# An efficient-attention kernel and two MLPs: the first attention units and MLP block 0 written in a list scheduler's order

## The chip, the core and the metric

The kernel runs on one core of one Trainium2 chip, as one program that the host launches once. The time is device microseconds of that core. Before the change it is 1768.31 us, the median of three runs (1767.80 to 1768.87).

## What is computed

Attention over 8 batches, 8 heads, 576 positions and 64 channels gives 4608 tokens of 512 channels; two gated MLPs (512 to 2048 to 512) follow.

```python
def _attn_ref(q, k, v):
    q_s = np.exp(q - np.max(q, axis=-1, keepdims=True))
    q_s = q_s / (np.sum(q_s, axis=-1, keepdims=True) + 1e-09)
    k_s = np.exp(k - np.max(k, axis=2, keepdims=True))
    k_s = k_s / (np.sum(k_s, axis=2, keepdims=True) + 1e-09)
    kv = np.einsum('bhsd,bhse->bhde', k_s, v)
    return np.einsum('bhsd,bhde->bhse', q_s, kv)

def _moe_ref(x, w_in, w_out):      # first MLP
    h = x @ w_in
    return (h * np.clip(h + 3.0, 0.0, 6.0) / 6.0) @ w_out

def _moe2_ref(x, w_in, w_out):     # second MLP
    h = x @ w_in
    return (h * (1.0 / (1.0 + np.exp(-h)))) @ w_out
```

## The kernel before

**Tiling.** The 4608 tokens are nine blocks of 512. Each MLP (a phase, `ph` 0 and 1) goes over the nine blocks `j`, and in each over sixteen slices `f` of 128 of the 2048 hidden channels: 288 steps `n` in all. A step is `mm1` (12 matmuls 128x512 into a PSUM tile `h`), `gate` on ScalarE and VectorE, and `mm2` (12 matmuls into the four accumulators `y0` to `y3`). The loop issues `mm2` one step late, so that PE has `mm1` of step n, then `mm2` of step n-1, while the gate of step n runs.

**Three products for one.** Every matmul operand is split into an upper part in fp32r and the remainder, and three products are summed. So each operand needs a ScalarE copy (upper) and a VectorE subtraction (lower): `gate` does it for g (L414, L415), `x_upper` and `x_lower` for x (L371, L376), and class `Conv` for the weights. A `Conv` of a raw 512 KB weight tile is two ScalarE multiplications (`begin`, L111 and L113, which write `fa` and `fr`), three VectorE operations on the bits (`bits`, L117, L121, L122), the ScalarE copy (`upper`, L136) and the VectorE subtraction (`lower`, L140). Block 0 of the first MLP needs 32 of them, a w_in and a w_out slice for each of its sixteen steps.

**Attention units.** A unit `u` is one block of tokens and one pair of heads; four units make the x of a block. A unit passes seven stages: `q_max` (L298) and `k_max` (L219 to L221), `q_sub` on GpSimd (L306) and `k_turn` on PE (L226), `k_diag`, `k_spread`, `q_exp`, `q_sum` (L321 to L323), `q_norm` on GpSimd (L328), `k_sub` (L247), `k_exp` (L257), `q_turn`, `q_upper` and `q_lower` (L336, L341, L346), `kv_mm`, `kv_sum`, `kv_upper`, `kv_lower` (L267, L275, L284, L290), `x_mm` (L361), `x_upper`, `x_lower`.

**What sets the order.** All is written in a manual schedule: each engine runs its instructions in the order in which the program issues them, and the framework adds only the waits for data and for free buffers. Units 0 to 3 are issued in a first loop (`for t in range(NP + 2)`, L505) that works on three units at a time, each one stage behind the next; the first three `Conv` and the first `mm1` stand at its end. Then the loop over steps (L564) issues, for each step, fixed pieces of the units that are due (`begin`, L549: units 4 to 7 begin at steps 0, 3, 6 and 9), the two `Conv` for step f + 2 while `ph == 0 and j == 0`, `mm1`, `gate`, and `mm2` of the step ahead. Both `Conv` of a step are begun at its start and ended (`upper`, `lower`) behind its gate. Loads go through SP's queue: five pairs of weight tiles at the start, later one pair per step, between the q, k and v of the units.

**Buffers.** `wts` holds sixteen w_in and sixteen w_out tiles. Its buffers first take the raw tiles of slices 0 to 12 and the q, k and v of units 2 and 3 (`early`, L463 to L472); a split tile takes the place of the oldest. Raw tiles 13 to 15 pass through the pool `raw` of two. `t2k` has six buffers of 2 KB for `fa`, `fr`, `r` and others, `g` two, `h` two, `pa` two.

## Time and profile before

| | |
|---|---|
| median of the runs | 1768.31 us |
| the profiled execution | 1766.78 us, its span 1765.1 us, the remaining 1.7 us lie outside the span |
| mean granted clock of TensorE | 0.987 of full speed |
| PE / PEld busy | 96% / 79% of the span |
| DVE / ACT / POOL busy | 45% / 34% / 4% |
| DMA | 125 MB, 71 GB/s over the span |

A row of a group of instructions gives line, engine, operation, the tile written and those read, the shape, and the count; behind the bar the busy time in us and the mean of one in ns; behind the second bar how long the engine stood idle just before them, and what ended it. A row of a timeline begins with the start and the duration in us from the start of the span. DVE is VectorE, ACT is ScalarE, POOL is GpSimd, SP is the engine that issues most DMAs; PEclk is the granted TensorE clock, where 1.00 is 2.4 GHz.

### The profile page before, as it was taken

To read this page: it belongs to the slowest core of one execution; us is meant where nothing else is said; L and a number is where in the kernel's file an instruction comes from. 1 tells how busy PE (TensorE), PEld (TensorE's weight loads), DVE (VectorE), ACT (ScalarE), POOL (GpSimd) and SP (SyncE) were. 2 spreads that over 40 slices of the span, in tenths; PEclk is the share of its full clock that TensorE was granted. 3 is DMA by queue.
4 is the path that set the end of the run, shared out by engine and by line. 5 is a ranking of instruction groups with operands and counts; after the bars stand their busy time and mean duration, and the time that the engine had idled before them with its cause. 6 is when DMAs were issued, how large, how long until landed. Compare 5 with 4: busy or idle time off the path is not lost.

```text
span 1765.1 us, 20277 instructions
## 1 busy us (share of the span) xinstructions
PE 1690.0 (96%) x7984; PEld 1386.6 (79%) x7984; DVE 801.5 (45%) x1450; ACT 600.9 (34%) x1046; POOL 76.8 (4%) x82
## 2 busy tenths in 40 slices
PE   3678899999999999999999999999999999999998
PEld 2456788888888888888888888888888888888887
DVE  6788655556565656555432323232323232332322
ACT  2555444444343434433322322222222222222222
POOL 2000000000000000000000000000000000000000
PEclk9888999999999999999999999999999999999999
DMA  9051522323232323312055201010101010101000
GB/s 282 31 182 32 147 81 81 105 86 105 80 110 81 114 84 104 98 60 78 25 193 201 84 1 48 1 48 1 48 1 48 1 48 1 48 1 48 9 16 24
DMA packets 108319, 125.06 MB, mean 71 GB/s; under 512 B 48320, under 2 KB 82112, under 8 KB 108224
## 3 DMA queue, kind: packets, MB, share of 16 engines
q1 hardware_dynamic: 105824, 123.17, 22.1%
q8 instruction: 63, 1.03, 0.2%
q10 hardware_dynamic: 2400, 0.59, 0.2%
q14 instruction: 32, 0.26, 0.0%
HBM read 88.08 MB, written 35.65 MB: 70 GB/s over the span
## 4 chain that ended last, share of the span: by engine, by line
PE 89%; DVE 6%; ACT 2%; DMA 2%; issue 1%; ACTq 0%; SPq 0%; DVEq 0%
PE h L391 43%; PE y L431 22%; PE y L429 20%; PE pa L361 2%; DVE fa L121 1%; PE pa L267 1%; DVE fa L122 1%; PE pa L336 1%; ACT fa L111 0%; DMA kbuf<-in_k_dram 0%; DVE r L404 0%; DVE fa L117 0%; DVE wo L140 0%; DVE g L415 0%; DMA qraw<-in_q_dram 0%
## 5 line engine op out<-in xcount | busy, mean ns | idle before, releaser
L391 PE MATMUL h<-x,wi 128*128 128x512 f32 x3456 | 847.9, 394 | 0.0
L391 PEld LDWEIGHTS h<-x,wi 128*128 128x128 f32 x3456 | 649.2, 190 | 135.8 <-DVE wi L140 0.4
L429 PE MATMUL y<-g,wo 128*128 128x512 f32 x1728 | 425.6, 396 | 0.1
L431 PE MATMUL y<-wo,g 128*128 128x512 f32 x1728 | 414.9, 389 | 0.0
L431 PEld LDWEIGHTS y<-wo,g 128*128 128x128 f32 x1728 | 324.4, 188 | 67.3
L429 PEld LDWEIGHTS y<-g,wo 128*128 128x128 f32 x1728 | 323.6, 190 | 67.7 <-ACT g L414 0.5
L409 DVE TENSOR_TENSOR r<-r,h 128x512 f32<-128x512 f32 x144 | 99.1, 688 | 455.3 <-ACT r L408 455.3
L415 DVE TENSOR_TENSOR g<-r,g 128x512 fp32r<-128x512 f32 x288 | 199.4, 692 | 146.5 <-ACT g L414 133.9
L414 ACT CAST g<-r 128x512 fp32r<-128x512 f32 x288 | 179.4, 623 | 250.8 <-DVE r L404 142.2
L408 ACT ACTIVATE r<-h 128x512 f32<-128x512 f32 x144 | 86.5, 601 | 468.2 <-PE h L391 468.2
L404 DVE SCALAR_TENSOR_TENSOR r<-r,h 128x512 f32<-128x512 f32 x144 | 98.8, 686 | 263.2 <-ACT r L403 263.2
L403 ACT ACTIVATE r<-h 128x512 f32<-128x512 f32 x144 | 86.3, 600 | 258.8 <-PE h L391 247.8
L361 PE MATMUL pa<-qT,kv 128*128 128x512 f32 (+7 forms) x192 | 40.7, 347 | 24.7 <-DVE kv L290 13.2
L121 DVE CUSTOM_DVE_ANT_0 fa<-fa,fr 128x1024 uint16<-128x1024 uint16 x64 | 53.7, 839 | 9.2 <-ACT r L403 0.5
L361 PEld LDWEIGHTS pa<-qT,kv 128*128 128x128 f32 x192 | 33.0, 207 | 30.3 <-ACT kv L284 12.2
L328 POOL TENSOR_TENSOR qe<-qe,qs 128x512 f32<-128x512 f32 x36 | 37.8, 1050 | 397.8 <-DVE qs L323 386.7
L306 POOL TENSOR_TENSOR qe<-qraw,qm 128x512 f32<-128x512 f32 x34 | 35.7, 1050 | 366.8 <-issue 287.7
L117 DVE TENSOR_SCALAR fa<-fa 128x512 uint32<-128x512 uint32 x64 | 29.4, 459 | 40.0 <-ACT fa L111 40.0
L257 ACT ACTIVATE ke<-ke 128x640 f32<-128x640 f32 x32 | 23.7, 741 | 58.8 <-DVE ke L247 58.8
L371 ACT CAST x<-pa 128x512 fp32r<-128x512 f32 x36 | 21.2, 588 | 38.3 <-PE pa L361 38.2
L284 ACT ACTIVATE kv<-pa,rs 64x64 fp32r<-64x64 f32 x56 | 17.5, 312 | 47.6 <-DVE rs L276 47.3
L267 PEld LDWEIGHTS pa<-vbuf,ke 128*64 128x64 f32 (+1 forms) x560 | 20.8, 136 | 12.2 <-issue 6.7
(80 smaller groups left out, 697.8 us busy)
## 6 DMA issues: line engine op xcount, KB each, us to landing
wd<-sp SPq DMA_DIRECT2D x32, 512.0 KB, 3.0
wi_raw<-in_moe_w_in_dram SPq DMA_DIRECT2D x19, 512.0 KB, 4.7
wo_raw<-in_moe_w_out_dram SPq DMA_DIRECT2D x19, 512.0 KB, 4.2
yd<-o SPq DMA_DIRECT2D x36, 256.0 KB, 2.7
yr<-yd SPq DMA_DIRECT2D x36, 256.0 KB, 3.0
out_dram<-o SPq DMA_DIRECT2D x36, 256.0 KB, 3.3
wi<-wd SPq DMA_DIRECT2D x16, 512.0 KB, 4.2
wo<-wd SPq DMA_DIRECT2D x16, 512.0 KB, 4.2
```

The lines of the kernel that those rows point to most:

```text
L121: nc.vector.tensor_tensor(out=au, in0=au, in1=self.r, op=ALU.add)
L267: nc.tensor.matmul(pk[d, 0 : D + 1], t[0:n, j, d], tv[0:n, j, h, :], start=(j == 0), stop=(j == KCH),)
L361: nc.tensor.matmul(pv[:, :, p0 : p0 + n], w[:, a, :], qT[:, c, :, p0 : p0 + n], start=(n_ == 0), stop=(n_ == 2),)
L391: nc.tensor.matmul(h, w[:, a, c, :], x[:, e, c, :], start=(c == 0 and n == 0), stop=(c == NC - 1 and n == 2),)
L403: nc.scalar.activation(r, h, AF.Relu, bias=3.0)
L404: nc.vector.scalar_tensor_tensor(out=r, in0=r, scalar=6.0, in1=h, op0=ALU.min, op1=ALU.mult)
L408: nc.scalar.activation(r, h, AF.Sigmoid)
L409: nc.vector.tensor_tensor(out=r, in0=r, in1=h, op=ALU.mult)
L414: nc.scalar.copy(g[:, 0], r)
L415: nc.vector.tensor_tensor(out=g[:, 1], in0=r, in1=f32(g[:, 0]), op=ALU.subtract)
L429: nc.tensor.matmul(y[c], w[:, a, cs], g[:, e, :], start=st, stop=sp)
L431: nc.tensor.matmul(y[c], g[:, e, cs], w[:, a, :], start=st, stop=sp)
```

## The change

The part of the program up to the last gate of block 0 is no longer written out as two loops. `first_block` makes a list of jobs (engine, assumed duration, priority, what it must wait for, which buffers it takes and gives back), and `Plan.run` goes through an assumed clock and puts out, at each moment and for each engine, the free job with the lowest key. The kernel's instructions are then issued in that order; no wait is added to hold an engine to the plan. The plan holds a tag `port`, which keeps POOL's tensor operations and certain DVE operations apart in its assumed time. `Conv.bits` and `gate` are cut into single operations so that they can be placed apart, and the loop over steps begins at step 16.

All 32 raw weight tiles now have a place in `wts`, so that each is split into the tile it lies in, and their loads stand in SP's queue without a step's work between them. The q, k and v of units 2 and 3 lie in `ahead`, the second buffer of the x tiles, which is free until x of block 1 is written. The same operations are done on the same data, with the same number of DMAs.

```diff
-        def bits(self):
+        def shift(self):
             au = self.a.bitcast(U32)
             nc.vector.tensor_scalar(
                 out=au, in0=au, scalar1=3, scalar2=None, op0=ALU.logical_shift_left
             )
+        def round(self):
+            au = self.a.bitcast(U32)
             nc.vector.tensor_tensor(out=au, in0=au, in1=self.r, op=ALU.add)
+        def sign(self):
+            au = self.a.bitcast(U32)
             nc.vector.scalar_tensor_tensor(
                 out=au, in0=self.high, scalar=0x80000000, in1=au,
                 op0=ALU.bitwise_and, op1=ALU.bitwise_or,
             )
+        def bits(self):
+            self.shift()
+            self.round()
+            self.sign()
...
+    class Gate:
+        def __init__(self, s):
+            self.s = s
+        def relu(self):
+            self.h = hp.pop(self.s)
+            self.r = tmp.tile([P, BLK], F32, tag="t2k", name="r")
...
-    EARLY = NF - 3
-    for u in range(2, NP):
-        kbuf[u] = wts.tile([P, 2, KCH + 1, D], F32, tag="wi", name="k_early")
-        vbuf[u] = wts.tile([P, KCH + 1, 2, D + 1], F32, tag="wo", name="v_early")
-        early["q", u] = wts.tile(
-            [P, 2, NCH, D], F32, tag="wi" if u % 2 else "wo", name="q_early"
-        )
-    for f in range(EARLY):
+    KB, VB, QB = 2 * (KCH + 1) * D, (KCH + 1) * 2 * (D + 1), 2 * NCH * D
+    ahead = xs.tile([P, 2 * NC * BLK], F32, tag="x", name="ahead")
+    for i, u in enumerate(range(2, NP)):
+        o = i * (KB + VB + QB)
+        kbuf[u] = ahead[:, o : o + KB].rearrange("p (h j d) -> p h j d", h=2, d=D)
+        vbuf[u] = ahead[:, o + KB : o + KB + VB].rearrange("p (j h d) -> p j h d", h=2, d=D + 1)
+        early["q", u] = ahead[:, o + KB + VB : o + KB + VB + QB].rearrange(
+            "p (h i d) -> p h i d", h=2, d=D
+        )
+    for f in range(NF):
...
+    class Plan:
+        PORT = "port"
+        def __init__(self, **tags):
+            self.jobs, self.tags = [], dict(tags, port=1)
+        def add(self, eng, us, key, fn, deps=(), take=(), give=(), port=False):
+            self.jobs.append(
+                (eng, us, key, fn, [d for d in deps if d is not None], list(take), list(give), port)
+            )
+            return len(self.jobs) - 1
...
+                for i in sorted(ready, key=lambda i: jobs[i][2]):
+                    eng, us, key, fn, deps, take, give, port = jobs[i]
+                    if at[i] > now + 1e-9 or busy.get(eng, 0.0) > now + 1e-9:
+                        continue
+                    need = take + ([self.PORT] if port else [])
+                    if any(self.tags[t] < need.count(t) for t in need):
+                        continue
+                    for t in need:
+                        self.tags[t] -= 1
+                    stop = now + us
+                    busy[eng] = stop
+                    if port:
+                        gives.append((stop, [self.PORT]))
+                    if eng in ("SP", "AQ"):
+                        fn, size = fn
+                        dma = max(dma, stop + 1.9) + size / 235e3
+                        stop = dma
+                    if give:
+                        gives.append((stop, give))
+                    end[i] = stop
+                    order.append(fn)
...
+    def first_block():
+        plan = Plan(a=2, h=2, g=2, qe=1, qT=1, ke=1, dg=1, m1=1, t2k=6, q=2, **{f"y{c}": 1 for c in range(NC)})
...
+            qm = add("DVE", 0.7, key(0), lambda: q_max(u), [n_q[u]])
+            km = add("DVE", 1.05, key(0), lambda: k_max(u), [n_k[u]], ["m1", "t2k"], ["t2k"], True)
+            if until <= 1:
+                return
+            kt = add("PE", 0.45, key(1), lambda: k_turn(u, pool), [km], [bank], ["m1"])
+            kd = add("DVE", 0.6, key(1), lambda: k_diag(u), [kt], ["dg"], [bank])
+            qs = add("POOL", 1.05, key(1), lambda: q_sub(u, nc.gpsimd), [qm], [qe], [], True)
...
+            mm = add(
+                "PE", 1.5, key(4), lambda: kv_mm(u, y_psum(u) if small else a_pool),
+                [kx, n_v[u]], [pkb], ["ke"],
+            )
+            kvmm[u] = mm
...
+        plan.tags["ke"] = 2
+        s0 = -30.0
+        load(0, s0, "k")
+        load(0, s0 + 0.1, "q")
+        load(0, s0 + 0.2, "v", "AQ")
+        load(1, s0 + 0.3, "k")
+        load(1, s0 + 0.4, "q")
+        load(1, s0 + 0.5, "v", "AQ")
+        for u in range(2, NP):
+            for i, what in enumerate("kqv"):
+                load(u, s0 + u + 0.1 * i, what)
+        for u in range(NP):
+            unit(u, lambda r, u=u: -20.0 + u - 0.01 * r)
...
+        raws, split = {}, {}
+        for f in range(NF):
+            for o in range(2):
+                raws[o, f] = add(
+                    "SP", 0.55, -10.0 + 0.9 * f + 0.4 * o + (0 if f < 4 else 3.0),
+                    (lambda f=f, o=o: load_w(0, f, o), 524288),
+                )
+        for f in range(NF):
+            for o in range(2):
+                c = Conv(0, f, o)
+                key = f - (1.6 if o else 2.2)
+                c0 = add("ACT", 1.35, key, c.begin, [raws[o, f]], ["t2k", "t2k"])
+                c1 = add("DVE", 0.45, key, c.shift, [c0], port=True)
+                c2 = add("DVE", 0.7, key, c.round, [c1], [], ["t2k"], True)
+                c3 = add("DVE", 0.72, key, c.sign, [c2], port=True)
+                c4 = add("ACT", 0.65, key, c.upper, [c3])
+                split[o, f] = add("DVE", 0.7, key, c.lower, [c4], [], ["t2k"], True)
...
+        for u in (NP, NP + 1):
+            loads(u, -6.5 + (u - NP) * 0.5)
+            unit(u, lambda r, u=u: begin[u] + r + 0.3)
...
+                m = add(
+                    "PE", 0.78, f - 0.5, lambda s=s, c=c: mm1(s, [c]),
+                    [split[0, f], xlow[c], m], ["h"] if c == 0 else [],
+                )
+            g = Gate(s)
+            g0 = add("ACT", 0.62, f - 0.45, g.relu, [m], ["t2k"])
+            g1 = add("DVE", 0.7, f - 0.45, g.times, [g0], [], ["h"])
+            g2 = add("ACT", 0.64, f - 0.45, g.upper, [g1], ["g"])
+            g3 = add("DVE", 0.7, f - 0.45, g.lower, [g2], [], ["t2k"], True)
+            if f < NF - 1:
+                last = add(
+                    "PE", 3.1, f + 0.55, lambda s=s: mm2(s), [g3, split[1, f], last],
+                    [f"y{c}" for c in range(NC)] if f == 0 else [], ["g"],
...
+        for i in range(2):
+            add("SP", 0.55, 14.0 + 0.5 * i, (lambda i=i: load_w(1, 0, i), 524288))
+        for fn in plan.run():
+            fn()
...
-        for u in range(NP):
-            load_q(u)
-            load_k(u)
-            load_v(u, nc.scalar if u < 2 else nc.sync)
...
+        first_block()
...
-        prev = None
-        for n, s in enumerate(steps):
+        prev = steps[NF - 1]
+        for n, s in list(enumerate(steps))[NF:]:
...
-            if ph == 0 and j == 0 and f + 2 < NF:
-                convs = [Conv(0, f + 2, 0), Conv(0, f + 2, 1)]
-            elif ph == 0:
+            if ph == 0:
...
-                if j == 0:
-                    if f + 5 < NF:
-                        load_w(0, f + 5, 0)
-                        load_w(0, f + 5, 1)
-                    if f >= NF - 2:
-                        load_w(1, 0, f - NF + 2)
```

**Places where the order moves.** The first is the start of the program on VectorE: the kernel before, from the first attention operation on (m is `k_max`, mx and dg `k_diag`, qs `q_sum`, ke `k_sub`, rs `kv_sum`; the numbers tell the buffers apart):

```order
L298 TENSOR_REDUCE qm_186<-qraw_150 128x8
L219 TENSOR_TENSOR m2_190<-kbuf0_94 128x256
L232 TENSOR_REDUCE mx_197<-ph_195 128x1
L321 TENSOR_REDUCE qs_204<-qe_188 128x8
L298 TENSOR_REDUCE qm_208<-qraw_157 128x8
L219 TENSOR_TENSOR m2_212<-kbuf1_96 128x256
L247 TENSOR_TENSOR ke_219<-kbuf0_94,ph_201 128x2x5x64
L346 TENSOR_TENSOR qT_228<-pa_223,qT_228 128x512
L232 TENSOR_REDUCE mx_231<-ph_217 128x1
L275 TENSOR_SCALAR rs_253<-pk_242 128x1
L298 TENSOR_REDUCE qm_264<-q_early_102 128x8
```

and after the change:

```order
L224 TENSOR_TENSOR m2_168<-kbuf0_94 128x256
L237 TENSOR_REDUCE mx_178<-ph_176 128x1
L303 TENSOR_REDUCE qm_186<-qraw_156 128x8
L252 TENSOR_TENSOR ke_189<-kbuf0_94,ph_184 128x2x5x64
L224 TENSOR_TENSOR m2_197<-kbuf1_96 128x256
L326 TENSOR_REDUCE qs_215<-qe_191 128x8
L280 TENSOR_SCALAR rs_223<-pk_203 128x1
L237 TENSOR_REDUCE mx_228<-ph_221 128x1
L252 TENSOR_TENSOR ke_250<-kbuf1_96,ph_237 128x2x5x64
L224 TENSOR_TENSOR m2_257<-ahead_100 128x256
L351 TENSOR_TENSOR qT_253<-pa_242,qT_253 128x512
```

The k chain of unit 0 now goes through before anything of unit 1, and `q_lower` of unit 0 (the line with qT), which stood right behind `k_sub` of unit 0, stands behind work of units 1 and 2.

The second is ScalarE in block 0, before, from `k_exp` of unit 4 to the `Conv` of the next step:

```order
L257 ACTIVATE ke_867<-ke_867 128x640
L341 CAST qT_891<-pa_885 128x512
L111 ACTIVATE fa_895<-wi_early_122 128x512
L113 ACTIVATE fr_896<-wi_early_122 128x512
L111 ACTIVATE fa_902<-wo_early_123 128x512
L113 ACTIVATE fr_903<-wo_early_123 128x512
L403 ACTIVATE r_922<-h_909 128x512
L414 CAST g_923<-r_922 128x512
L136 CAST wi_929<-fa_895 128x512
L136 CAST wo_932<-fa_902 128x512
```

and after, around the same unit's `k_exp`:

```order
L111 ACTIVATE fa_671<-wi_early_111 128x512
L113 ACTIVATE fr_672<-wi_early_111 128x512
L409 ACTIVATE r_688<-h_652 128x512
L147 CAST wi_692<-fa_635 128x512
L262 ACTIVATE ke_690<-ke_690 128x640
L424 CAST g_717<-r_688 128x512
L346 CAST qT_733<-pa_719 128x512
L111 ACTIVATE fa_736<-wo_early_112 128x512
L113 ACTIVATE fr_737<-wo_early_112 128x512
L147 CAST wo_748<-fa_648 128x512
L111 ACTIVATE fa_755<-wi_early_113 128x512
```

A `Conv` is now begun one `Conv` ahead of the one that is being ended (`fa_671` is begun before `fa_635` is copied), and the attention copies stand between begun ones.

The third is SP's queue before, at the q of unit 6 (`qraw_588`):

```order
L193 DMA qraw_588<-in_q_dram 16x2x256
L193 DMA qraw_588<-in_q_dram 112x2x256
L94 DMA wi_early_120<-in_moe_w_in_dram 128x4x256
L88 DMA wo_early_121<-in_moe_w_out_dram 128x1024
L167 DMA kbuf0_94<-in_k_dram 128x2x256
```

and after (`qraw_608`):

```order
L94 DMA wi_early_131<-in_moe_w_in_dram 128x4x256
L88 DMA wo_early_132<-in_moe_w_out_dram 128x1024
L94 DMA wi_raw_479<-in_moe2_w_in_dram 128x4x256
L88 DMA wo_raw_486<-in_moe2_w_out_dram 128x1024
L198 DMA qraw_608<-in_q_dram 16x2x256
L198 DMA qraw_608<-in_q_dram 112x2x256
L172 DMA kbuf0_94<-in_k_dram 128x2x256
```

The q and k of unit 6, which stood behind the raw tiles of seven of the sixteen slices, now stand behind all sixteen and the first two tiles of the second MLP; 26 weight tiles lie between the loads of unit 5 and it.

## Rows read from the trace of the kernel before

**Rows 1.** The page: the span, and PE's busy share in tenths, 40 slices.

```profile
span 1765.1 us, 20277 instructions
...
PE   3678899999999999999999999999999999999998
```

**Rows 2.** Timeline of PE: start, duration, line, operation, count, idle time before.

```profile
53.99 7.60 PE L391 MATMUL h<-x,wi 128*128 128x512 f32 x24
...
190.97 4.26 PE L391 MATMUL h<-x,wi 128*128 128x512 f32 x12
...
203.97 3.02 PE L391 MATMUL h<-x,wi 128*128 128x512 f32 x12
```

**Rows 3.** Busy time by stage: PE, PEld, DVE, ACT, POOL, clock, DMA, GB/s.

```profile
5.00:54.00 49.00, 20.54 (x121) 14.30 (x122) 32.84 (x70) 16.14 (x30) 7.94 (x8) 0.96 0.77 237
54.00:203.60 149.60, 114.44 (x508) 89.11 (x507) 121.01 (x227) 81.92 (x148) 10.57 (x10) 0.86 0.32 95
203.60:1765.00 1561.40, 1555.04 (x7358) 1283.18 (x7356) 645.32 (x1144) 502.85 (x868) 56.42 (x54) 1.00 0.20 63
```

**Rows 4.** Waits of DVE from 5 to 54 us: total, times, longest.

```profile
DVE qT L346 <- ACT qT L341: 5.9, 4, 1.8
...
DVE rs L275 <- PE pk L267: 2.3, 2, 1.4
...
DVE mx L232 <- PE ph L226: 0.6, 1, 0.6
```

**Rows 5.** Waits of DVE from 54 to 203.6 us.

```profile
DVE fa L117 <- ACT fa L111: 10.8, 8, 1.8
DVE r L404 <- ACT r L403: 4.5, 2, 2.5
...
DVE fa L121 <- ACT fr L113: 0.3, 2, 0.2
```

**Rows 6.** Timelines of ACT and DVE around one such wait.

```profile
145.94 0.74 ACT L257 ACTIVATE ke<-ke 128x640 f32<-128x640 f32 x1 [1.65 <-DVE ke L247]
...
147.05 0.67 ACT L111 ACTIVATE fa<-wi_early 128x512 f32<-128x512 f32 x1
...
147.76 0.43 DVE L117 TENSOR_SCALAR fa<-fa 128x512 uint32<-128x512 uint32 x1 [1.25 <-ACT fa L111]
```

**Rows 7.** Timelines of POOL and DVE at one POOL operation, and the same DVE operations alone.

```profile
80.15 1.05 POOL L328 TENSOR_TENSOR qe<-qe,qs 128x512 f32<-128x512 f32 x1 [16.11 <-DVE qs L323]
...
80.44 1.31 DVE L121 CUSTOM_DVE_ANT_0 fa<-fa,fr 128x1024 uint16<-128x1024 uint16 x1
...
82.95 0.69 DVE L121 CUSTOM_DVE_ANT_0 fa<-fa,fr 128x1024 uint16<-128x1024 uint16 x1
...
155.19 0.29 DVE L220 TENSOR_TENSOR m<-m 128x128 f32<-128x128 f32 x1
```

**Rows 8.** Groups of DVE: L121 from 54 to 203.6 us, the others up to 54 us.

```profile
L121 DVE CUSTOM_DVE_ANT_0 fa<-fa,fr 128x1024 uint16<-128x1024 uint16 x30 | 23.9, 796 | 4.5 <-ACT r L403 0.5 <-ACT fr L113 0.3
...
L220 DVE TENSOR_TENSOR m<-m 128x128 f32<-128x128 f32 x4 | 3.4, 852 | 0.1
...
L221 DVE TENSOR_TENSOR m<-m,k_early 128x128 f32<-128x128 f32 x2 | 2.0, 1014 | 0.1
```

**Rows 9.** PE's timeline: `mm2` after two idle times of different length.

```profile
98.32 0.45 PE L226 MATMUL pa<-ident,m 128*128 128x128 f32 x1 [5.32 <-DVE rs L275]
98.42 4.51 PE L429 MATMUL y<-g,wo 128*128 128x512 f32 x12
...
127.33 0.30 PE L226 MATMUL pa<-ident,m 128*128 128x128 f32 x1 [2.22 <-DVE rs L275]
127.38 2.99 PE L429 MATMUL y<-g,wo 128*128 128x512 f32 x12
```

**Rows 10.** DMA from 0 to 110 us, 40 slices of 2.75 us: GB/s, and weight tiles to landing.

```profile
GB/s 63 304 289 248 233 158 350 366 399 393 400 272 193 153 367 342 7 0 0 0 0 0 0 36 286 158 0 0 0 0 0 0 113 268 344 338 366 37 0 0
...
wi_early<-in_moe_w_in_dram SPq DMA_DIRECT2D x11, 512.0 KB, 6.1
```

More of the change, by code (lines that the diff above doesn't have):

```diff
@@ L143, in lower @@
                 nc.sync.dma_start(wd[self.key[1], self.key[2]], f32(t))
-        def all(self):
-            self.begin()
-            self.bits()
-            self.upper()
-            self.lower()
     def load_split(f, o):
@@ L394, in mm1, with times, upper, lower @@
                 )
-    def gate(s, act=None, dve=None):
-        ph, j, f = s
-        h = hp.pop(s)
-        r = tmp.tile([P, BLK], F32, tag="t2k", name="r")
-        g = gs.tile([P, 2, BLK], F32R, tag="g", name="g")
-        if ph == 0:
-            nc.scalar.activation(r, h, AF.Relu, bias=3.0)
-            nc.vector.scalar_tensor_tensor(
-                out=r, in0=r, scalar=6.0, in1=h, op0=ALU.min, op1=ALU.mult
-            )
-        else:
-            nc.scalar.activation(r, h, AF.Sigmoid)
-            nc.vector.tensor_tensor(out=r, in0=r, in1=h, op=ALU.mult)
-        if act:
-            act()
-        if dve:
-            dve()
-        nc.scalar.copy(g[:, 0], r)
-        nc.vector.tensor_tensor(out=g[:, 1], in0=r, in1=f32(g[:, 0]), op=ALU.subtract)
-        gt[s] = g
+    class Gate:
[4 more added lines that the diff above has]
+            self.r = tmp.tile([P, BLK], F32, tag="t2k", name="r")
+            if self.s[0] == 0:
+                nc.scalar.activation(self.r, self.h, AF.Relu, bias=3.0)
+            else:
+                nc.scalar.activation(self.r, self.h, AF.Sigmoid)
+        def times(self):
+            r, h = self.r, self.h
+            if self.s[0] == 0:
+                nc.vector.scalar_tensor_tensor(
+                    out=r, in0=r, scalar=6.0, in1=h, op0=ALU.min, op1=ALU.mult
+                )
+            else:
+                nc.vector.tensor_tensor(out=r, in0=r, in1=h, op=ALU.mult)
+        def upper(self):
+            self.g = gt[self.s] = gs.tile([P, 2, BLK], F32R, tag="g", name="g")
+            nc.scalar.copy(self.g[:, 0], self.r)
+        def lower(self):
+            nc.vector.tensor_tensor(
+                out=self.g[:, 1], in0=self.r, in1=f32(self.g[:, 0]), op=ALU.subtract
+            )
+    def gate(s, between):
+        g = Gate(s)
+        g.relu()
+        g.times()
+        between()
+        g.upper()
+        g.lower()
     def mm2(s):
@@ L481, in a_pool, with run @@
         return a_psum(None)
+    class Plan:
[7 more added lines that the diff above has]
+            return len(self.jobs) - 1
+        def run(self):
+            jobs, n = self.jobs, len(self.jobs)
+            busy, end, order, now = {}, [None] * n, [], 0.0
+            left = set(range(n))
+            gives = []
+            waits = [len(j[4]) for j in jobs]
+            users = [[] for _ in jobs]
+            for i, j in enumerate(jobs):
+                for d in j[4]:
+                    users[d].append(i)
+            at = [0.0] * n
+            ready = [i for i in range(n) if not waits[i]]
+            dma = 0.0
+            while left:
+                gives.sort()
+                while gives and gives[0][0] <= now + 1e-9:
+                    for tag in gives.pop(0)[1]:
+                        self.tags[tag] += 1
+                started = False
+                for i in sorted(ready, key=lambda i: jobs[i][2]):
[19 more added lines that the diff above has]
+                    order.append(fn)
+                    left.discard(i)
+                    ready.remove(i)
+                    for v in users[i]:
+                        waits[v] -= 1
+                        same = jobs[v][0] == eng
+                        at[v] = max(at[v], stop + (0.0 if same else 0.1))
+                        if not waits[v]:
+                            ready.append(v)
+                    started = True
+                if not left:
+                    break
+                if not started:
+                    later = [g[0] for g in gives] + [at[i] for i in ready] + list(busy.values())
+                    later = [t for t in later if t > now + 1e-9]
+                    assert later, [jobs[i][:3] + (jobs[i][5],) for i in ready]
+                    now = min(later)
+            self.span = now
+            return order
```

125 lines of the change are left out of this document (70 added, 55 removed).

## The prediction

> **What bounds the kernel now.** I read the page first. Its row of PE's busy share [rows 1] shows two stages: nine tenths or more from the sixth slice to the last but one, and 3 to 8 tenths in the first five slices, the first 220 us or so of 1765.1. So the question is how long the first stage is. PE's timeline [rows 2] gives its marks: the first `mm1` at 53.99 us, unbroken work from 190.97, and `mm1` of step 16, the first of block 1, at 203.97. I call that last moment the handover. The table by stage [rows 3] shows what lies on either side. Behind the handover PE is busy 1555.0 of 1561.4 us at full clock with work that the change leaves as it is, so each microsecond by which the handover comes earlier is one off the time. Ahead of it DVE is the busiest engine: 121.0 of 149.6 us from 54 us on, against 114.4 for PE (at a mean clock of 0.86) and 81.9 for ACT. From 5 to 54 us it is busy 32.8 of 49.0.
>
> What DVE waits for is in its two lists of waits. From 5 to 54 us eight waits sum to 14.6 us, from the 5.9 behind `q_upper` down to 0.6 [rows 4]. From 54 us to the handover another eight sum to 22.8 [rows 5], and 10.8 of that is the first operation of a step's `Conv`, waiting for ACT's multiplication. The timelines show why [rows 6]: ACT's L111 needs nothing from DVE, but stands in ACT's order behind `k_exp` of an attention unit, which itself waited 1.65 us for DVE. DVE then stood 1.25 us.
>
> DVE also loses time to POOL. While POOL's 1.05 us operation ran, L121 took 1.31 us and not 0.69 [rows 7]. The groups give the sum [rows 8]: 30 times L121 at 796 ns instead of 690 is 3.2 us; four L220 at 852 ns instead of the 290 of [rows 7] are 2.2; two L221 at 1014, against the same 290, are 1.4. Together 6.8 us.
>
> So the 198.6 us from 5.0 to 203.6 are 153.9 of DVE at work (6.8 of it lost to POOL), 37.4 of waits, and some 7 of the small gaps between dependent operations, which stay.
>
> **The change part by part.** No operation is added or removed; what moves is when each is issued. The sum is therefore over DVE's idle and lost time.
>
> *(a) The first four units.* Before, each unit's `q_upper`, `kv_upper` and sums are waited for with nothing else issued in between; now three units' stages alternate on DVE. The waits of 14.6 us shrink to those of the first unit, which has little beside it while the others' data is on its way: `rs` 2.3 and the smaller ones of `qs`, `mx` and `k`, 0.6 to 0.7 each, 4.2 in all. Gain 10.4; bounds 0 and 14.6.
>
> *(b) Block 0.* A `Conv` is begun on ACT one ahead, and DVE's four operations of it stand apart from each other with gates between. That removes the cause of the 10.8 us. The 4.5 of `times` behind the gate's ScalarE operation [rows 5] I leave in: these are two waits in the last two steps, where no `Conv` is left to fill and PE is what is waited for. Of 22.8 us, 18.3 go; bounds 0 and 22.8. In-order waits can move to other operations, and that is the main rival.
>
> *(c) POOL beside DVE.* The plan keeps the two apart in its assumed time only. I leave a quarter of the 6.8 us, gain 5.1. Bounds: all of it gone, or all 18 POOL tensor operations of this stage (two for each of nine units) hitting at the worst price seen, 1014 minus 290 ns, 13.0 us, which is 6.2 more than now. I take a value near the first end because the order as issued puts other DVE work beside POOL; how far the chip drifts from it is the open point.
>
> *(d) Weights in place, and the loads.* The raw tiles no longer wait for a buffer of the pool of two, and no wait of DVE in the two lists ended with the DMA of a weight tile, so this gives nothing by itself. It is what lets 26 tiles of 512 KB, 13.6 MB, go ahead of unit 6's q. When the queue had tiles to move it ran at 350 to 400 GB/s [rows 10], 39 us at the lower. Unit 5's loads can be out by 36 us (as before), so unit 6's q goes out near 75 us. DVE comes to it in the middle of its block 0 list, by this forecast near 105. Cost 0, cover 30 us.
>
> *(e) Units 2 and 3 in `ahead`.* The first write of x for block 1 must wait until unit 3's q, k and v are read, in the first 40 us; that x is unit 4's and comes much later. Cost 0.
>
> *(f) PE.* The first `mm1` comes earlier by (a) and the L220 and L221 part of (c), 10.4 plus 3.6, so near 40 us. Its 114.4 us of work would be done at 154, so DVE still sets the handover, with 16 us to spare.
>
> Sum: 10.4 + 18.3 + 5.1 = 33.8 us. Handover at 170. The profiled execution took 1766.8 us; minus 33.8 is 1733.0. The median of the runs shown is 1.5 us above that execution, so the forecast is **1734.5 us**. Its own range: with all three at their good bound (14.6 + 22.8 + 6.8 = 44.2) 1724; with half of (a) and (b) and nothing of (c), 18.7, it is 1750. What a measurement of this kernel can tell from no change is about 0.2%, 3.5 us.
>
> **The rivals.**
>
> *Waits that only change place.* DVE, ACT and PE each run in order, and the plan's durations are assumptions. If an operation comes late where the plan had it early, everything behind it stands, and block 0 could lose as much as now. Then (a) and (c) alone remain, 15.5 us: 1753, with 1750 to 1760 around it. For it: ACT now has the gate's operation, which waits for PE, between the multiplications and copies of two `Conv`, so a late `mm1` stops both. Against it: DVE has more ready work per step than the time that ACT's two copies take.
>
> *TensorE's clock.* PE's `mm2` took 4.51 us after an idle time of 5.32 and 2.99 us after one of 2.22 [rows 9]; 0.86 is the mean clock of the stage. If PE now waits a little in every step and stays at the low level (1.2 GHz), 31 sets of 12 at 4.5 us, with about 12 for attention, make 152 us behind the start at 40: handover at 192, gain 12, time 1756. Against it: the idle time per step shrinks, and 2.22 us did no harm.
>
> *The loads of unit 6 come too late: slower than before.* They stand behind 26 tiles. If the queue moved one tile per 6.1 us, the time to landing of a single tile [rows 10], 26 take 159 us, q goes out at 195 instead of 75, 90 us after DVE wants it; DVE stands at `q_max` with `Conv` and gates queued behind it, PE behind those: 1824. It begins to hurt under 13.6 MB / 69 us = 197 GB/s, and makes the kernel slower than before under 13.6 / 103 = 132. Against it: the 350 to 400 in [rows 10].
> The Trainium skill (DMA: Bandwidth & Descriptors, Queues, rings and completion order) says that each DMA engine takes a queue's descriptors in ring order. By that rule unit 6's q can overtake none of the 26, as this rival has it; no row here shows an overtaking.
>
> *POOL hits DVE every time.* Nothing holds the engines to the plan. With 18 hits at 0.72 us each (bad bound of (c)) DVE loses 13.0 us and not 1.7: 1746. For it: POOL's operations become free when DVE ends a sum, so DVE is always in the middle of something. Against it: the same was so before, and 18 operations cost 6.8 us.
> The Trainium skill (SBUF — State Buffer, Who interferes with whom) says that a DVE operation with two SBUF inputs and a POOL operation that reads SBUF exclude each other for the whole instruction. By that rule each hit could cost POOL's full 1.05 us, 18.9 us in all, and the time would be near 1752. The row agrees that DVE is held, but L121 lost 0.62 us, not 1.05 [rows 7].
>
> *No change.* The order does alter the program, as the places quoted show. But the assumed clock might be so far off that the lists interlock as badly as before: 1768.
>
> **How the numbers follow.** Forecast 0.68, waits that change place 0.15, POOL 0.05, clock 0.05, no change 0.03, late loads 0.04. The range starts at 1723, the good bound, and ends at 1755, which takes in the forecast's own range, POOL's rival and half of the first: 0.8 in all. Faster: 0.68 + 0.15 + 0.05 + 0.05 = 0.93; same 0.03; slower 0.04.
>
> **What would show it.** Right: `mm1` of step 16 near 170 us (164 to 180), the first `mm1` near 40, DVE's waits ahead of the handover near 9 us in place of 37, `fa` behind ACT's L111 nearly gone from the list, L121 back at 0.69 us, and the same 1555 us of PE behind the handover. Wrong: a first `mm1` past 46 us (a), a list with new waits of 15 us or more between 40 us and the handover (b), PE busy nine tenths at a clock under 0.8 in block 0, a wait of `q_max` for its DMA, or PE idle behind the handover.

## The result and the profile after

The changed kernel takes **1723.05 us** (median of 4 runs, 1722.27 to 1724.06) against 1768.45 (4 runs, 1767.80 to 1768.87): a ratio of **0.9744, interval 0.9727 to 0.9761**. That is 45.4 us less; the forecast was 33.8 less. The profiled execution took 1723.36 us with a span of 1721.6, where before it was 1766.78 with 1765.1.

The page, for [rows 1]: the span, and PE's busy share in tenths.

```profile
span 1721.6 us, 20220 instructions
...
PE   5888999999999999999999999999999999999998
```

PE is at nine tenths from the fifth slice to the last but one; before, five slices held 3 to 8, and now four hold 5 to 8. PE's timeline, for [rows 2]:

```profile
33.52 2.09 PE L396 MATMUL h<-x,wi 128*128 128x512 f32 x3 [0.46 <-ACT wi L147]
35.40 1.48 PE L366 MATMUL pa<-qT,kv 128*128 128x512 f32 x3
...
157.38 0.69 PE L341 MATMUL pa<-ident,qe 128*128 128x128 f32 x4 [2.03 <-POOL qe L333]
157.80 4.57 PE L396 MATMUL h<-x,wi 128*128 128x512 f32 x12
```

The first `mm1` stands at 33.52 us instead of 53.99, and `mm1` of step 16, the handover, at 157.80 instead of 203.97: 46.2 us earlier. The table by stage (PE, PEld, DVE, ACT, POOL, clock, DMA, GB/s), for [rows 3]:

```profile
5.00:33.52 28.52, 18.34 (x118) 12.69 (x118) 25.24 (x61) 16.22 (x31) 8.45 (x8) 0.85 0.96 285
33.52:157.80 124.28, 107.56 (x515) 79.54 (x515) 120.79 (x236) 87.14 (x149) 11.68 (x10) 0.98 0.44 145
157.80:1721.60 1563.80, 1557.55 (x7356) 1283.91 (x7354) 644.36 (x1142) 500.82 (x868) 56.45 (x54) 1.00 0.20 63
```

In block 0 DVE is now busy 120.8 of 124.3 us. Behind the handover the span holds 1563.8 us, 2.7 more than the 1561.1 before. So 2.7 of the 46.2 are given back behind the handover. 1.5 of them lie in its first set: `q_turn` of unit 8 stands ahead of `mm1` in PE's order, PE stood 2.03 us for POOL's `q_norm` (this stop lies ahead of 157.80 and is in the 46.2 already), and the 12 matmuls behind it took 4.57 us against 3.02 in [rows 2]. The granted clock from 157.38 to 161.30 us was 0.56; from there on it was 1.00. The other 1.2 are spread over later steps. All of DVE's listed waits from 5 us to the handover, for [rows 4, 5]:

```profile
DVE qs L326 <- ACT qe L321: 1.0, 1, 1.0
DVE mx L237 <- PE ph L231: 0.6, 1, 0.6
DVE x L381 <- ACT x L376: 0.4, 1, 0.4
DVE qm L303 <- DMA qraw<-in_q_dram: 0.3, 1, 0.3
```

They were 37.4 us and are 2.3, and all of them end ahead of the first `mm1`: none lies in block 0.

**DVE's ledger.** Between 5 us and the handover each row of DVE's timeline was put against the start of the next. "Overlap" is the next one starting before this one's end, "small gap" at the end or up to 0.25 us behind it, "wait" later than that; us, and pairs in brackets.

| | durations | overlap | small gaps | waits |
|---|---|---|---|---|
| before | 164.6 | -10.0 (120) | 9.1 (137) | 35.6 (32) |
| changed | 160.1 | -14.1 (174) | 3.9 (109) | 1.7 (3) |
| difference | -4.5 | -4.1 | -5.2 | -33.9 |

The four differences make 47.7 us. The handover moved 1.5 less: the ledgers begin 0.5 us apart, and DVE's last operation ends 0.6 us ahead of the handover now, where before it ended 0.4 past it. The columns of overlap and small gaps are what the forecast had left as it was. The timeline of DVE before, where a `Conv` is followed by the gate:

```profile
111.40 0.42 DVE L117 TENSOR_SCALAR fa<-fa 128x512 uint32<-128x512 uint32 x1
111.95 0.69 DVE L121 CUSTOM_DVE_ANT_0 fa<-fa,fr 128x1024 uint16<-128x1024 uint16 x1
112.68 0.69 DVE L122 SCALAR_TENSOR_TENSOR fa<-wo_early,fa 128x512 uint32<-128x512 uint32 x1
113.29 0.68 DVE L404 SCALAR_TENSOR_TENSOR r<-r,h 128x512 f32<-128x512 f32 x1
```

and of the changed kernel:

```profile
112.84 0.42 DVE L117 TENSOR_SCALAR fa<-fa 128x512 uint32<-128x512 uint32 x1
113.30 0.69 DVE L124 CUSTOM_DVE_ANT_0 fa<-fa,fr 128x1024 uint16<-128x1024 uint16 x1
113.91 0.68 DVE L151 TENSOR_TENSOR wo<-fa,wo 128x512 fp32r<-128x512 f32 x1
114.51 0.68 DVE L427 TENSOR_TENSOR g<-r,g 128x512 fp32r<-128x512 f32 x1
115.11 0.68 DVE L128 SCALAR_TENSOR_TENSOR fa<-wi_early,fa 128x512 uint32<-128x512 uint32 x1
```

Read the starts. L122 depends on L121 and starts 0.73 us after it, 0.04 past its end. L404 depends on neither and starts 0.61 after L122, 0.08 before that one's end. So the same operation costs DVE about 0.11 us more where its neighbour is its producer. Also, L121 before started 0.55 after L117 (median 0.56 of 30) and now L124 starts 0.46 after it, in each of 26 such pairs. Both additions depend on the shift in front of them. Before, the gap between the two was 0.14 us or more in all 32 pairs, and in all 32 the trace has an instruction of DVE in it that only waits for a semaphore (EVENT_SEMAPHORE, 21 ns, at 111.86 us here; the views leave such instructions out); in the 26 pairs of the changed kernel there is none, and the gap is 0.03 or 0.04. In the other runs, too, the gap is 0.14 to 0.16 us wherever such an instruction stands in it, and 0.03 or 0.04 where a shift is followed by its own addition without one. That instruction waits for DVE's own count, that is for the shift, while the addition itself waits for ACT's second multiplication. The multiplication being late is not the cause: in 23 of the 32 pairs it had ended before the shift ended (here at 110.41 us). So a second thing to wait for cost the addition 0.10 us, whether or not that thing was late. Why the new order needs one wait only, no run shows.

### The profile page after: what moved, and what is told of

Its sections match the earlier page's. It is cut to its first block, busy times and chain, and to the rows that moved or that the text cites. A ratio compares the mean times of both kernels' runs of the same rounds, so it can differ in the third digit from the quotient of the medians.

```text
span 1721.6 us, 20220 instructions
## 1 busy us (share of the span) xinstructions
PE 1683.4 (98%) x7984; PEld 1376.1 (80%) x7984; DVE 793.1 (46%) x1450; ACT 604.2 (35%) x1046; POOL 77.9 (5%) x82
## 4 chain that ended last, share of the span: by engine, by line
PE 90%; ACT 0%; ACTq 0%; issue 0%
PE h L396 44%; PE y L453 23%; PE y L451 20%; PE pa L366 1%; PE pa L272 1%; PE pa L341 1%; PE pa L244 0%; PE pa L231 0%; ACT o L465 0%; ACTq L865 0%
## 5 line engine op out<-in xcount | busy, mean ns | idle before, releaser
L396 PEld LDWEIGHTS h<-x,wi 128*128 128x128 f32 x3456 | 643.9, 188 | 147.0 <-DVE wi L151 10.2
L451 PE MATMUL y<-g,wo 128*128 128x512 f32 x1728 | 421.0, 392 | 0.0
L124 DVE CUSTOM_DVE_ANT_0 fa<-fa,fr 128x1024 uint16<-128x1024 uint16 x64 | 51.3, 801 | 5.4
L117 DVE TENSOR_SCALAR fa<-fa 128x512 uint32<-128x512 uint32 x64 | 28.4, 443 | 29.9 <-ACT fa L111 29.9
L366 PE MATMUL pa<-qT,kv 128*128 128x512 f32 (+7 forms) x192 | 37.4, 328 | 1.2 <-DVE qT L351 0.7
L341 PE MATMUL pa<-ident,qe 128*128 128x128 f32 x144 | 23.8, 291 | 7.0 <-POOL qe L333 7.0
```

The source lines that it names most:

```text
L124: nc.vector.tensor_tensor(out=au, in0=au, in1=self.r, op=ALU.add)
L341: nc.tensor.transpose(pq[:, i * P : (i + 1) * P], t[:, i, :], ident)
L366: nc.tensor.matmul(pv[:, :, p0 : p0 + n], w[:, a, :], qT[:, c, :, p0 : p0 + n], start=(n_ == 0), stop=(n_ == 2),)
L396: nc.tensor.matmul(h, w[:, a, c, :], x[:, e, c, :], start=(c == 0 and n == 0), stop=(c == NC - 1 and n == 2),)
L451: nc.tensor.matmul(y[c], w[:, a, cs], g[:, e, :], start=st, stop=sp)
```

## The experiments

All times are medians beside runs of the kernel before on the same chip (medians 1767.98 to 1768.45 us). "First" is the first `mm1`, "handover" `mm1` of step 16, both in us from the start of the span; the last handover is counted off in a row that joins 6 matmuls of step 15 with the 12. The "lead-in" is the stretch ahead of the first `mm1`.

| kernel | us | ratio, interval | first | handover |
|---|---|---|---|---|
| changed | 1723.05 | 0.9744, 0.9727 to 0.9761 | 33.5 | 157.8 |
| buffers alone | 1767.47 | 0.9997, 0.9988 to 1.0006 | 54.7 | 204.7 |
| lead-in alone | 1750.30 | 0.9898, 0.9884 to 0.9913 | 33.2 | 186.1 |
| block 0 alone | 1741.94 | 0.9849, 0.9833 to 0.9866 | 55.3 | 178.6 |
| no port rule | 1725.90 | 0.9762, 0.9748 to 0.9775 | 35.1 | 161.7 |
| bits tied | 1724.98 | 0.9756, 0.9743 to 0.9769 | 32.3 | 161.2 |
| apart | 1717.28 | 0.9712, 0.9699 to 0.9725 | 33.2 | 152.7 |
| no POOL | 1726.42 | 0.9763, 0.9750 to 0.9776 | 35.7 | 162.9 |
| fused | **1708.10** | **0.9660, 0.9646 to 0.9674** | 33.1 | 143.8 |
| before, fused | 1756.73 | 0.9938, 0.9924 to 0.9951 | 54.1 | 193.8 |
| fused and apart | 1710.29 | 0.9672, 0.9659 to 0.9685 | 32.5 | 145.3 |
| the same, unit 8 later | 1712.39 | 0.9683, 0.9669 to 0.9696 | 33.9 | 145.8 |

**Buffers alone.** Before's loops with the new tiles.

```diff
-    EARLY = NF - 3
...
+    ahead = xs.tile([P, 2 * NC * BLK], F32, tag="x", name="ahead")
...
+                for f in range(4, NF):
+                    load_w(0, f, 0)
+                    load_w(0, f, 1)
...
-                    if f + 5 < NF:
-                        load_w(0, f + 5, 0)
-                        load_w(0, f + 5, 1)
```

> Before's hand-written order, with the changed kernel's buffers alone: all 32 raw weight tiles of the first MLP in the weight pool, units 2 and 3 in the second x tile, and the weight loads issued ahead as there. Theory (the order brings the gain; no wait of DVE before ended with a weight tile's DMA): 1768 us, within 3, first mm1 at 54, DVE waits ahead of the handover 37 us as before. Rival (buffers and early loads bring a good part): 1750 or less, first mm1 or handover earlier by 15 us or more.

It took 1767.47 us, no measurable change, with nearly the same waits in block 0:

```profile
DVE fa L117 <- ACT fa L111: 10.8, 8, 1.8
DVE r L404 <- ACT r L403: 4.7, 2, 2.8
```

So (d) and (e) are worth nothing by themselves, as forecast; the order is what brings the gain.

**Lead-in alone, and block 0 alone.** The first keeps the list for units 0 to 3 and step 0 and puts before's loop behind it; the second has before's loop ahead of the list. The lines are from the edit of the first.

```diff
-        for f in range(NF):
+        for f in range(2):
             for o in range(2):
                 c = Conv(0, f, o)
...
-        for n, s in list(enumerate(steps))[NF:]:
+        for n, s in enumerate(steps):
```

> Only the lead-in (units 0 to 3, the Conv of f = 0 and 1, mm1 of step 0) is listed by the scheduler; block 0 is written in before's loop; the changed kernel's buffers. Theory (the two halves are separate stretches of DVE and add up): first mm1 at 33 to 36 us, block 0 as long as before (150 us), handover near 184, time 1748. Rival (time won in the lead-in is given back in block 0, whose convoy of waits does not shorten because PE or ACT start it in another state): handover past 192, time above 1756.

> Only block 0 is listed by the scheduler; the lead-in is before's hand-written loop; the changed kernel's buffers. Theory: first mm1 at 54 us, block 0 as in the changed kernel (124 us), handover near 178, time 1745. Rival (the block's gain rests on Conv work that the scheduled lead-in had already put in): block 0 of 135 us or more, time above 1755.

The lead-in alone is 17.7 us faster, block 0 alone 26.0; together 43.7, and the changed kernel has 45.4. The halves add up to within 2 us; with the lead-in alone the stretch from first `mm1` to handover is 152.9 us where it was 150.0, so 2.9 of its gain are lost again there. Their lists of DVE's waits in block 0 show why; first the lead-in alone (before's loop):

```profile
DVE fa L117 <- ACT fa L111: 10.8, 8, 1.8
DVE r L416 <- ACT r L409: 5.7, 2, 3.5
DVE g L427 <- ACT g L424: 3.6, 8, 0.7
```

then block 0 alone (the two longest of four):

```profile
DVE x L387 <- ACT x L382: 1.7, 1, 1.7
DVE kv L301 <- ACT kv L295: 0.8, 1, 0.8
```

All four, 3.9 us, end ahead of 63 us, in what this kernel's hand-written loop still issues; the list behind it has no wait of DVE. The waits behind L111 and those of the gate go with the list and stay with the loop. Neither rival of these two runs came about.

**No port rule, no POOL.** In the first the plan no longer keeps POOL and DVE apart; in the second DVE does POOL's 18 tensor operations.

```diff
-                    need = take + ([self.PORT] if port else [])
+                    port = False
+                    need = take
```

> The changed kernel with a list built without the rule that keeps POOL's operations and DVE's port operations apart. Theory (the rule saves part of the time that DVE loses beside POOL): DVE's loss goes from 4.8 us (the groups of the changed kernel) back to before's 7.7 or a little more, handover 3 us later, 1726 us. Rival A (the chip drifts from the plan, so the rule decides nothing): 1723 within 1, the same loss. Rival B (without it nearly every one of the 18 operations of POOL hits at 0.72): loss 13, 1731.

It took 1725.90 us, 2.9 more than the changed kernel, as the theory had it; the intervals of the two ratios overlap, but no run of the one lies in the range of the other. DVE's loss is larger than expected: the groups up to the handover give 9.9 us, most of it in groups such as these two, which now read

```profile
L151 DVE TENSOR_TENSOR wi<-fa,wi 128x512 fp32r<-128x512 f32 x16 | 15.0, 935 | 0.0
...
L239 DVE TENSOR_SCALAR dg<-ident,mx 128x128 f32<-128x128 f32 x9 | 4.5, 495 | 0.3
```

with 685 and 287 ns alone: 4.0 and 1.9 us. The 4.8 and 7.7 of the expectation leave out some operations that are counted here (L224 in the changed kernel, L117 and L219 before). Counted row by row, as what a DVE operation took beyond the median of its kind away from POOL, the loss is 8.7 us in 14 rows before, 5.2 in 8 rows in the changed kernel and 9.8 in 15 rows without the rule. So the rule, which holds only in assumed time, still saves 4.6 us of DVE, and without it the handover comes 3.9 later.

```diff
-            qs = add("POOL", 1.05, key(1), lambda: q_sub(u, nc.gpsimd), [qm], [qe], [], True)
+            qs = add("DVE", 0.69, key(1), lambda: q_sub(u, nc.vector), [qm], [qe], [], True)
...
-            qn = add("POOL", 1.05, key(2), lambda: q_norm(u, nc.gpsimd), [qa], [], [], True)
+            qn = add("DVE", 0.69, key(2), lambda: q_norm(u, nc.vector), [qa], [], [], True)
```

> The changed kernel with POOL's 18 tensor operations ahead of the handover (q_sub and q_norm of units 0 to 8) given to DVE at 0.69 us, planned so. Theory (DVE sets the handover, and POOL costs it only the 4.8 us that its groups show): 18 at a pitch of 0.61 to 0.72 are 11 to 13 us more, less 4.8, so 6 to 8 more than the changed kernel: 1729 to 1731. Rival (POOL costs DVE and the chain of a unit more than the groups show): 1725 or less.

It took 1726.42 us, 3.4 more: between theory and rival. The 18 operations take DVE 12.3 us by their groups (679 to 683 ns) and the loss beside POOL is gone, yet the handover comes only 5.1 us later. The ledger of this kernel says where the rest went: durations 7.0 more, overlaps and small gaps 0.8 less, waits 0.3 less, and DVE's last operation now ends 0.2 us past the handover, not 0.6 ahead of it. Of the 5.1 another 1.9 are missing in the time, because 1561.9 us and not 1563.8 lie behind the handover: above all, the set that ran at the lower clock in the changed kernel runs at full clock here. So POOL is worth 5.1 us ahead of the handover, against the 6 to 8 expected.

**Bits tied, and apart.** Two lists that differ in how many neighbours on DVE depend on each other: the first ties a `Conv`'s three bit operations together, the second delays an operation behind its producer so that another can go between.

```diff
-                c1 = add("DVE", 0.45, key, c.shift, [c0], port=True)
-                c2 = add("DVE", 0.7, key, c.round, [c1], [], ["t2k"], True)
-                c3 = add("DVE", 0.72, key, c.sign, [c2], port=True)
+                c3 = add("DVE", 1.87, key, c.bits, [c0], [], ["t2k"], True)
```

> The changed kernel with the shift, the addition and the sign of a Conv as one job of the list, so that they follow each other on DVE: 131 neighbours on DVE depend on each other there, in place of 115 in the changed kernel and 142 before. Theory (a dependent neighbour starts 0.03 us after its producer's end, an independent one 0.08 before it; the order as such does not need the three apart): 16 more of them at 0.11 us are 1.8, so 1725 us. Rival (taking the Conv apart is what lets DVE fill its waits): new waits of 8 us or more in block 0, 1731 or above.

```diff
-                        at[v] = max(at[v], stop + (0.0 if same else 0.1))
+                        at[v] = max(at[v], stop + 0.1)
```

> The changed kernel with a list in which an operation that depends on the one before it on its own engine becomes ready 0.1 us after that one's end, so that an independent one goes first: 96 dependent neighbours on DVE in place of 115. Theory (0.11 us for each): 2.1 us less, 1721. Rival (what goes first is less urgent, and that costs as much or more): 1723 or above.

The first took 1724.98 us, the second 1717.28. The expectations counted neighbours by names in the order; the trace counts pairs with a small gap: 109 in the changed kernel, 131 with the bits tied, 68 apart. Times 0.11 that is 2.4 us more and 4.5 less; the handovers lie 3.4 later and 5.1 earlier. Overlap and small gaps together go from -10.2 to -6.9 and to -14.0 us. So the first came out as expected, and the second expectation had the mechanism and undercounted it. Taking a `Conv` apart matters little for the waits: with its three operations tied DVE's are 2.2 us by the ledger, where the changed kernel has 1.7.

**Fused.** One DVE operation less in each `Conv`, in the changed kernel and in the kernel before.

```diff
-            nc.scalar.mul(self.r, low, 2.0**-29)
+            nc.scalar.activation(self.r, low, AF.Copy, bias=-0.4999, scale=0.9999 * 2.0**-29)
...
-            nc.vector.tensor_scalar(
-                out=au, in0=au, scalar1=3, scalar2=None, op0=ALU.logical_shift_left
-            )
...
-            nc.vector.tensor_tensor(out=au, in0=au, in1=self.r, op=ALU.add)
+            nc.vector.scalar_tensor_tensor(
+                out=au, in0=au, scalar=3, in1=self.r,
+                op0=ALU.logical_shift_left, op1=ALU.bitwise_or,
+            )
```

> The changed kernel with one DVE operation less in each Conv: the shift by three bits and the integer addition become one scalar_tensor_tensor (shift, or), with ACT's low part cut off instead of rounded; the list is built with that operation at 0.7 us. Theory (DVE's work sets the handover): 32 operations less at a start-to-start time of 0.46 to 0.56 us are 15 to 18 us less for DVE; PE, busy 104 of 121 us in block 0, becomes the next bound near 143 to 147, so handover near 145, time 1709 to 1713, DVE with new idle time. Rival (PE or ACT already sets it, DVE is only full because it is given work early): handover 155 or later, time 1720 or above.

> The kernel before, in its own order, with the shift and the addition of a Conv as one DVE operation (32 operations less). Theory (in the hand-written order block 0 is set by a ring of waits between ACT, PE and DVE, so that DVE work taken out turns into waits): 1758 to 1764 us, DVE's waits ahead of the handover up from 37 by about half of what is taken out. Rival (DVE's work is the bound in either order): the same 14 to 15 us as in the changed kernel, 1753.

In the changed kernel it brings 15.0 us more, 1708.10, and the handover goes to 143.75: DVE does set it. This is the fastest kernel of the study. In the kernel before the same edit brings 11.5, between the two expectations: its longest wait in block 0 now reads

```profile
DVE fa L117 <- ACT fr L113: 16.8, 12, 2.4
```

in place of the 10.8 behind L111, and the listed waits of block 0 sum to 28.1 us where they were 22.8. By the ledger of the whole stretch durations, overlaps and small gaps are 16.8 us less, waits 6.5 more, and the handover comes 10.2 earlier. So some 40% of what was taken out turned into waits, and the rest was gained.

**Fused and apart, and unit 8 later.** The second begins unit 8 at step 16.

```diff
-            begin[j * NP + pr] = 3 * pr if j == 1 else (j - 1) * NF + 4 * pr - 3
+            begin[j * NP + pr] = 3 * pr if j == 1 else NF + 3 * pr if j == 2 else (j - 1) * NF + 4 * pr - 3
```

> The fused Conv of e5 with the list of e7 (an operation that depends on its neighbour becomes ready 0.1 us after it). Theory (both act on DVE's work ahead of the handover, but PE, busy 110 of 117 us in e5's block 0, is nearly full): 1 to 3 us less than e5, 1705 to 1707. Rival A (they add up as if DVE were alone): 5 to 6 less, 1702. Rival B (PE already sets the handover): 1708 as e5.

> e8 with unit 8 begun at step 16 (behind the handover, units 8 to 11 three steps apart) instead of step 13. Theory (behind the handover DVE has room, ahead of it has not): unit 8's first three stages are some 4 us of DVE ahead of the handover; PE allows about 2 to 4 of it: 2 to 3 us less than e8. Rival A (PE sets the handover alone): as e8 within 1. Rival B (units 8 to 11 now come late for block 2, which waits): above e8.

Both missed: 1710.29 and 1712.39, 2.2 and 4.3 us above the fused kernel. That one was timed on another chip, beside its own runs of before, and the intervals of the ratios overlap, so a loss is likely and not certain; the handovers are 1.5 and 2.1 us later too. That the expected gains did not come is certain. PE's waits in block 0, listed for the fused kernel, sum to 7.2 us; with "apart" they are 10.0, led by

```profile
PE h L391 <- DVE r L411: 2.8, 3, 1.4
PE pa L336 <- DVE ke L247: 2.2, 1, 2.2
```

and with unit 8 later PE stops behind the handover, where it did not in the kernel before, the changed and the fused one:

```profile
155.15 0.30 PE L226 MATMUL pa<-ident,m 128*128 128x128 f32 x1 [1.00 <-DVE m L221]
```

But PE is not the whole of it. With "apart" DVE, too, is still nearly full (busy 107.9 of 112.7 us in block 0), and its ledger against the fused kernel's reads: overlaps and small gaps 2.0 us less, durations 2.0 more, waits 1.7 more. The durations are POOL: row by row 11 DVE operations lose 7.9 us beside it, where 7 lost 4.9. So the neighbours gave 2.0 us, but with this list DVE met POOL more often and once waited 3.0 us for PE; which of the two decides was not run apart. With unit 8 later it is plainer: DVE's last operation ends 4.6 us ahead of the handover, so DVE has room, and still the handover is not earlier. There DVE time saved bought nothing; PE's waits in block 0 sum to 8.8 us, 1.2 of them for a weight tile's DMA. PE was busy 103.3 of the 110.7 us of the fused kernel's block 0, so at most 7.4 are left there.

## Why the prediction was right, and where its sizes were off

The mechanism was the forecast one: DVE sets the handover, its idle time was the order's doing, and the time follows the handover (46.2 and 45.4 us earlier). The size was not: the sum is 11.5 us short (1734.5 against 1723.05). The result lies inside the range by 0.05 us, two of its four runs lie below, and the handover at 157.8 missed the sign that the prediction set for it (164 to 180); that the range held is luck. The gain is past the sum of all good bounds (44.2), so a term was missing.

- **Small gaps "which stay": the step that failed.** They did not stay. With the overlaps they are worth 9.3 us in the ledger: 28 small gaps fewer and 54 overlaps more. Nor were they gaps "between dependent operations" alone: of the 9.1 us before, 4.3 lie in front of 31 additions whose second wait is an instruction of its own, 1.6 are short waits for other engines, and only 2.9 are plain gaps of 0.03 us behind a producer. An estimate from the mean gaps: the second waits give 3.2 us, 19 dependent neighbours fewer give 2.2 at 0.117 each, and most of the rest are operations that had waited for another engine and now follow an independent one. Bits tied and apart moved the dependent neighbours in both directions, and the handover with them.
- **(a) the first four units.** Forecast gain 10.4 and a first `mm1` near 40; the waits went from 14.6 to 2.3, and it stands at 33.5. Besides the waits, DVE does 25.2 us of work ahead of it, not the 32.8 of [rows 3]. 2.3 of the difference are less loss beside POOL; the rest the step overlooked. The plan cuts `mm1` into four chunks, so the first run at 33.52 while `x_mm` of unit 3 follows at 35.40 and `q_lower` of unit 3 at 34.79, and the w_out `Conv` of step 0 and the last operation of its w_in `Conv` come behind the first chunk.
- **(b) block 0.** Forecast 18.3 of 22.8; all went, which is this term's own good bound. The 4.5 of `times` [rows 5] were kept because "no `Conv` is left to fill" the last two steps and PE is waited for. That reading was wrong: with the old loop and a scheduled lead-in they are 5.7, with the list they are gone.
- **(c) POOL beside DVE.** Forecast 6.8 to 1.7. The 6.8 left out some operations (L117, L219 and one more L221): row by row the loss was 8.7 us and is 5.2, so the gain was 3.5 and not 5.1. Eight DVE operations are still held, where 14 were and the rival had 18; the dearest hit cost 0.80 us, none POOL's full 1.05. `k_diag`, which carries no `port` in the plan and lost nothing before, now reads 407 ns instead of 286. The groups from 5 us to the handover, for [rows 8]:

```profile
L124 DVE CUSTOM_DVE_ANT_0 fa<-fa,fr 128x1024 uint16<-128x1024 uint16 x32 | 22.8, 714 | 1.0
...
L225 DVE TENSOR_TENSOR m<-m 128x128 f32<-128x128 f32 x8 | 3.8, 476 | 0.3
L239 DVE TENSOR_SCALAR dg<-ident,mx 128x128 f32<-128x128 f32 x9 | 3.7, 407 | 0.3
```

- **(d), (e)** cost 0, as forecast; the buffers alone changed nothing. Unit 6's q went out at 64.70 us and DVE read it at 97.99, a cover of 33 us where 30 were forecast (75 and 105). The DMA row from 0 to 110 us in 40 slices, for [rows 10], stands near 400 GB/s from the fifteenth slice to the twenty-sixth, 38.5 to 71.5 us, so the rival of the late loads had no ground:

```profile
GB/s 53 237 287 189 202 223 206 366 401 402 378 228 187 215 369 406 406 404 400 406 402 402 403 398 394 399 264 144 0 0 3 80 84 57 0 0 26 69 0 0
```
- **(f) PE to spare.** Forecast 16 us. Taking work from DVE moved the handover by 14 (fused), and no run moved it further.
- **Behind the handover** nothing was to change; 2.7 us were lost there, 1.5 of them in a set of matmuls at the lower clock. Without the port rule and without POOL PE stands 1.64 and 1.91 us at the same place, but the set behind it runs at full clock, and 1562.3 and 1561.9 us are left of the span. The other 1.2 gather in small pieces up to step 112 or so; they stand in the lead-in alone and in "apart" too (1562.3 and 1562.2 us behind the handover), where PE does not stop, so they belong to the new program and not to the handover. Their cause stays open.

So by the ledger: waits 33.9 in place of 28.7, durations 4.5 for 5.1 (3.5 of them are POOL's), neighbours 9.3 for 0, the ends and what lies behind the handover -4.2 for 0: 43.5 us between the two spans. The rival of the changing places had its condition met (ACT's orders do mix gate and `Conv`) and its price not: no listed wait of DVE is left in block 0. Whether ACT's order or DVE's own did more for that was not run apart. The clock was 0.98 in block 0, against the rival that had it low.

## What to carry to other kernels

On an engine that sets the pace, add up starts, not durations: what an operation costs depends on whether its neighbour produced its input and on how many things it waits for, and reordering changes both. A list made at build time with coarse durations was enough to fill such an engine here, without anything on the chip that held it to the plan. Once the engine is full, less work on it helps (fused), and so do fewer dependent neighbours (apart); the two together did not add up, and an order made for one engine has to be looked at again for the others.

## What the hardware showed

Some DVE operations, when they are issued behind a running POOL operation, are held for nearly all that is left of it, however short they are themselves. POOL's and DVE's timelines in the changed kernel:

```profile
17.42 1.04 POOL L333 TENSOR_TENSOR qe<-qe,qs 128x512 f32<-128x512 f32 x1 [2.99 <-DMA ahead<-in_v_dram]
19.52 1.10 POOL L311 TENSOR_TENSOR qe<-ahead,qm 128x512 f32<-128x512 f32 x1 [1.06 <-issue]
```

```profile
17.46 1.08 DVE L239 TENSOR_SCALAR dg<-ident,mx 128x128 f32<-128x128 f32 x1
...
19.75 1.01 DVE L225 TENSOR_TENSOR m<-m 128x128 f32<-128x128 f32 x1
...
23.87 0.29 DVE L239 TENSOR_SCALAR dg<-ident,mx 128x128 f32<-128x128 f32 x1
```

L239 takes 0.29 us alone; issued 0.04 after POOL's operation it ended at 18.54, 0.08 after that one's end at 18.46. L225 ended 0.14 after POOL's. The loss is what is left of the POOL operation less 0.14 to 0.21 us (0.79 of 1.00 and 0.72 of 0.87 here), not a fixed price; the 0.62 of [rows 7] was a meeting with 0.76 left. Not every operation is held: in the changed kernel 44 DVE operations run beside one of POOL's 18, and 36 of them take their usual time, among them those that read a PSUM tile (L252 took its 0.81 us from 25.66, with POOL at work from 25.33 to 26.38) and the reductions of an SBUF tile (L303). Where the DVE operation is the first, POOL's takes longer: 1.31 us at 62.35, begun 0.23 behind a DVE operation of 0.64.
The Trainium skill (SBUF — State Buffer, Who interferes with whom) speaks of a lock held for the whole instruction and counts `tensor_scalar` among those that can take part; both agree with these rows.

PE's set of 12 matmuls at the handover took 4.57 us behind an idle time of 2.03, and with block 0 alone 4.58 behind 2.04; it took 3.00 behind 1.64 and behind 1.91 (no port rule, no POOL). But [rows 9] show 2.99 behind 2.22. The granted clock was 0.56 from PE's restart to 161.30 us in the first case and 0.59 over the set with block 0 alone, so mostly the lower level of 1.2 GHz, and 1.00 in the other three. So the length of the idle time alone does not tell which level of the clock follows; this was not taken further.
